# Decay bias by matmul, swapped keys out of the transpose, and one transpose of the probabilities per item, in an attention, SwiGLU and top-1 expert kernel

## The chip, the cores and the metric

The kernel runs on one core of a Trainium2 chip. The time is device microseconds (us) of one execution; the kernel before was timed three times. The profile is that of one further execution.

## What is computed

The inputs of the attention are q, k and v of 4 batches, 8 heads, 576 positions and 64 columns, and a decay f per position. The reference, cut to what matters:

```python
scores = scale * np.matmul(q, k.transpose(0, 1, 3, 2))
cum = np.cumsum(np.log(np.clip(f, 0.0001, 1.0)), axis=-1)
decay = cum[:, :, :, None] - cum[:, :, None, :]
scores = np.where(causal, -1000000000.0, scores + decay)
attn = softmax(scores)
x = np.matmul(attn, v)            # 2304 tokens of 512
x = (silu(x @ w_gate) * (x @ w_val)) @ w_out
x = top1_moe(x, gate, w1, w2)     # 8 experts
```

Within a row of the softmax the term of the query position is a constant, so only the term of the key position has to be subtracted from the scores.

## The kernel before

**Three stretches.** The attention goes by pairs of heads (16 pairs, 4 in each batch). Each pair has four items (`items`, L236): two heads times two groups of query rows; group 0 has the row blocks 0 to 2 and group 1 the row blocks 3 and 4. A slot (`slot`, L439) issues part 1 of item i, part 2 of item i-1 and the product with v of item i-2, and, by its place in the pair, the preparation of the next pair. In the first stretch (18 slots, about 165 us) the slots are mixed with the decoding and splitting of the weights, which come as 8-byte numbers. In the middle stretch (to about 612 us) the 46 slots left are mixed with units of the SwiGLU layer (`unit_g`, `unit_v`, `unit_o`), at a pace that `pace` (L1119) sets. After it come the remaining units, the routing and the experts, which the change doesn't touch.

**Order.** Every engine takes its instructions in the order of its own queue. That order is chosen when the kernel is built, by a planner that estimates when each instruction could start. All plain transfers and all DMA transposes of the attention are issued from the queue of SP.

**Preparation of a head** (`prep`, L200). q and k are scaled to f16 and split in a high and a low part: for each of the two, ScalarE writes the high part (L207) and VectorE the rest (L208). One DMA transpose (L210) turns the 10 blocks of 128 x 128 into `qkt`, with the high parts in partitions 0 to 63 and the low ones in 64 to 127. For the cross products high times low, VectorE copies the two halves of the transposed keys to swapped partitions (`ksw`, L214 and L215). The cumulated log decay of the head is fetched from `cum_d` in HBM, spread over 128 partitions by the transfer (`cb`, L218, 288 KB), and GpSimd multiplies it by the scale of the pair (L219).

**Part 1** (`part1`, L260). For each of the three column ranges of an item, `score` (L240) makes two matmuls, one with `qkt` (L244) and one with `ksw` (L246). In the first three batches (`inner`) a third one (L250) adds the causal mask of the diagonal block. VectorE then subtracts `cb` and takes the row maximum in one pass (L310). In the last batch there is no mask matmul: GpSimd adds the mask to `cb` for the diagonal blocks (L290), and the pass is cut in two where the diagonal block starts. ScalarE makes the bias of the exponential (L316) and the exponentials (L320).

**Part 2** (`part2`, L333). VectorE rounds the probabilities to f16 (L342), GpSimd makes the rest of the split (L345, L356), and a DMA transpose (L359) turns them: one of 9 blocks for an item of group 0, two of 7 and 9 blocks for an item of group 1. There are four f16 buffers of 9 blocks (`p16s`) and three transposed ones (`pt`).

**Product with v** (`pv`, L364): 40 matmuls per head (L380), each with one transposed block as the weights.

Of the kernel before, what the change touches and what calls it, by code (L numbers as in the profile page):

```python
# [7 lines left out]
F32 = mybir.dt.float32  # L8
# [13 lines left out]
MB = 3  # L22
# [6 lines left out]
def kernel(  # L29
# [36 lines left out]
    cum_d = dram.tile([B * H, S], F32, name="cum_d")  # L66
# [8 lines left out]
    masked = const.tile([128, 128], BF16, name="masked")  # L75
# [8 lines left out]
    rg = const.tile([128, KD, 32], F32, name="rg")  # L84
    sel = const.tile([128, NE], F32, name="sel")
# [11 lines left out]
    def consts():  # L97
# [5 lines left out]
        vec.tensor_scalar(out=masked, in0=maskgt, scalar1=-MASKED, scalar2=None, op0=ALU.mult)  # L103
# [18 lines left out]
        vec.tensor_single_scalar(out=sel, in_=sel_i, scalar=0.0, op=ALU.is_equal)  # L122
        vec.memset(rg, 0.0)
# [20 lines left out]
    NQK, NV, NPB, NBLK = 3, 1, 4, 9  # L144
# [6 lines left out]
    cb_p = at.enter_context(tc.tile_pool(name="cb", bufs=2))  # L151
# [4 lines left out]
    pt_p = at.enter_context(tc.tile_pool(name="pt", bufs=3))  # L156
# [24 lines left out]
    def scales(P):  # L181
        am = st_p.tile([128, 2], F32, tag="am", bufs=2, name="am")
        jk = qks_p.tile([128, 2, NCH, 2, D], F16, tag="qks", name="jk")
# [12 lines left out]
        stt[P] = (sc, c)  # L196
# [3 lines left out]
    def prep(P, hh):  # L200
        sc, c = stt[P]
        qks = qks_p.tile([128, 2, NCH, 2, D], F16, tag="qks", name="qks")
        for a in range(2):
            src = qk_in[(2 * P + a) % NQK][:, hh]
            s1 = sc[:, 0, a:a + 1]
            hi, lo = qks[:, a, :, 0, :], qks[:, a, :, 1, :]
# [3 lines left out]
        sp.dma_start_transpose(  # L210
            out=qkt.rearrange("p a (c t) -> p (a c) t", t=128), in_=qks.rearrange("p a c h d -> p (a c h d)")
        )
# [3 lines left out]
        cb = cb_p.tile([128, S], F32, tag="cb", name="cb")  # L216
        b, h = P // NP, 2 * (P % NP) + hh
        sp.dma_start(out=cb, in_=cum_d[b * H + h:b * H + h + 1, :].to_broadcast([128, S]))  # L218
        gp.tensor_tensor(out=cb, in0=cb, in1=c[:, 1:2].to_broadcast([128, S]), op=ALU.mult)  # L219
        heads[P, hh] = (qkt, ksw, cb)  # L220
# [19 lines left out]
    def score(ps, o, hd, j, k0, k1, inner):  # L240
        qkt, ksw, _ = hd
# [3 lines left out]
        d0, d1 = max(k0, 128 * j), k1 if inner else max(k0, 128 * j)  # L245
# [3 lines left out]
        if d1 > d0:  # L249
            pe.matmul(  # L250
                out=ps[:, o + d0 - k0:o + d1 - k0], lhsT=negid, rhs=maskgt[:, d0 - 128 * j:d1 - 128 * j],
                start=False, stop=True, skip_group_check=True,
            )
# [3 lines left out]

    stile = {}

    def part1(i):  # L260
        P, (hh, g) = i // 4, items[i % 4]
        hd = heads[P, hh]
        cb = hd[2]
        sc, c = stt[P]
        mx = st_p.tile([128, 8], F32, tag="mx", name="mx")
        inner = P < MB * NP
# [19 lines left out]
        if not inner:  # L286
            for m in range(nt):
                k0 = max(64, 128 * (base + m))
                k1 = 128 * (base + m) + 128
                gp.tensor_tensor(  # L290
                    out=sts[m][:, k0 - 64:k1 - 64], in0=cb[:, k0 - 64:k1 - 64], in1=masked[:, k0 - k1 + 128:], op=ALU.add
                )
        for grp in groups:
            ps = ps_s.tile([128, 512], F32, tag="s", name="ps")
            o = 0
            for j, k0, k1 in grp:
                score(ps, o, hd, j, k0, k1, inner)
                o += k1 - k0
            o = 0
            for j, k0, k1 in grp:  # L300
# [3 lines left out]
                d0 = k1 if inner else min(max(k0, 128 * j), k1)  # L304
                for a, b, bias in ((k0, d0, cb), (d0, k1, sts[m])):
                    if a < b:
                        left[m] -= b - a
                        x = m if not left[m] else nx
                        nx += left[m] > 0
                        vec.tensor_tensor_reduce(  # L310
                            out=sts[m][:, a - 64:b - 64], in0=ps[:, o + a - k0:o + b - k0], in1=bias[:, a - 64:b - 64],
                            scale=1.0, scalar=init, op0=ALU.subtract, op1=ALU.max, accum_out=mx[:, x:x + 1],
                        )
                        init = seen[m] = mx[:, x:x + 1]
# [13 lines left out]
    def p16_of(i, m):  # L328
        n, g = 6 * (i // 4), items[i % 4][1]
        n += i % 4 if g == 0 else 2 * (i % 4 - 1) + m  # L330
        return p16s[n % NPB].rearrange("p a t -> p (a t)"), 128 * OFF[m] if g == 0 else 0

    def part2(i):  # L333
# [4 lines left out]
        for ms in SUB[g]:  # L338
# [1094 lines left out]
```

## Time and profile before

| what | value |
|---|---|
| median of 3 runs | 1080.13 us (1072.58 to 1081.8) |
| the profiled execution | 1090.63 us |
| its span in the profile | 1088.5 us |
| TensorE busy | 880.6 us, 81% of the span |
| VectorE busy | 677.0 us, 62% |
| ScalarE busy | 537.0 us, 49% |
| GpSimd busy | 458.3 us, 42% |
| moved by DMA | 149.55 MB |

In the profile PE is TensorE's matmuls, PEld its weight loads, DVE is VectorE, ACT ScalarE, POOL GpSimd; SPq is the queue of SP, which issues transfers. L310 is line 310 of the kernel. A duration of one matmul includes its passage through the array, so matmuls overlap; how far apart they start tells what one costs.

### The profile page before, as it was taken

The page shows a single profiled execution, that of the slowest core. Times are in us where ns is not written, and L with a number is a line of the kernel's source. Part 1 is how long each engine was busy: PE and PEld are TensorE (multiplying, and loading weights), DVE is VectorE, ACT ScalarE, POOL GpSimd, SP SyncE. Part 2 cuts the span into 40 slices and gives each one's busy share as a digit, 9 for nine tenths or more (in the row PEclk, how much of TensorE's full clock was granted, in tenths as well). Part 3 has the DMA queues.
Part 4 walks back from the last instruction along what each step waited for, and adds up shares of the span by engine and source line. Part 5 has one row for each costly group of instructions (what it writes and reads, how often), then busy time and mean ns, then how long its engine had stood idle before and what let it go on. Part 6 is the DMA issues. An engine that isn't in the chain of part 4 may idle for free. (4 is left out here: it accounts for less than half of the span.)

```text
span 1088.5 us, 19531 instructions
## 1 busy us (share of the span) xinstructions
PE 880.6 (81%) x6789; PEld 726.5 (67%) x6789; DVE 677.0 (62%) x1946; ACT 537.0 (49%) x1160; POOL 458.3 (42%) x544
## 2 busy tenths in 40 slices
PE   1444448887976859899788899999877998999995
PEld 1333337765855648677667678888767887898994
DVE  4899799586675757777587542233334776665450
ACT  5877778464555636546264332222213645554441
POOL 2487676555344634466477412222215732110111
PEclk9995558998987979999989999999988999999998
DMA  8899889257778897767567360102328996555420
GB/s 222 186 228 221 189 171 216 63 121 158 166 102 155 144 127 155 148 108 147 84 103 155 45 194 11 40 1 39 59 48 207 255 218 190 167 181 164 173 100 31
DMA packets 298584, 149.55 MB, mean 137 GB/s; under 512 B 259697, under 2 KB 272113, under 8 KB 298484
## 3 DMA queue, kind: packets, MB, share of 16 engines
q1 hardware_dynamic: 294144, 137.83, 57.7%
q0 software_dynamic: 4096, 10.24, 3.9%
q8 instruction: 54, 0.88, 0.4%
q14 instruction: 46, 0.38, 0.2%
q10 hardware_dynamic: 244, 0.22, 0.1%
HBM read 91.06 MB, written 10.38 MB: 93 GB/s over the span
## 5 line engine op out<-in xcount | busy, mean ns | idle before, releaser
L490 PE MATMUL g<-xr,wg 128*128 128x256 f16 x1296 | 166.4, 282 | 18.9 <-ACT xr L433 10.5
L490 PE MATMUL v<-xr,wv 128*128 128x256 f16 x1296 | 170.1, 283 | 1.8 <-DVE t L523 1.2
L490 PEld LDWEIGHTS <-wv 128*128 128x128 f16 x1296 | 129.6, 103 | 32.9 <-issue 11.4
L490 PEld LDWEIGHTS <-wg 128*128 128x128 f16 x1296 | 125.1, 101 | 38.3 <-issue 16.9
L345 POOL TENSOR_TENSOR p<-st,p 128x128 f16<-128x128 f32 (+3 forms) x128 | 111.9, 880 | 45.1 <-DVE p L342 34.8
L530 POOL TENSOR_TENSOR lo<-t,hi 128x512 fp32r<-128x512 f32 x54 | 71.1, 1316 | 138.4 <-ACT hi L529 123.3
L380 PE MATMUL px<-vs,pt 128*128 128x64 f16 x1280 | 62.8, 207 | 65.1 <-DMA pt<-p 56.8
L380 PEld LDWEIGHTS <-pt 128*128 128x128 f16 x1280 | 55.6, 108 | 80.8 <-DMA pt<-p 64.2
L320 ACT ACTIVATE st<-st,nb,c 128x64 f32<-128x64 f32 (+4 forms) x160 | 102.7, 643 | 2.0
L342 DVE CAST p<-st 128x64 f16<-128x64 f32 (+4 forms) x160 | 74.4, 484 | 19.7 <-ACT st L320 16.2
L356 POOL TENSOR_TENSOR p<-st,p 128x64 f16<-128x64 f32 (+1 forms) x128 | 57.0, 448 | 54.0 <-issue 34.7
L529 ACT ACTIVATE hi<-t 128x512 fp32r<-128x512 f32 x54 | 33.7, 624 | 85.1 <-DVE t L523 85.1
L977 POOL DMA_INDIRECT out_dram<-o,ix x24 | 25.4, 1057 | 114.9 <-ACT o L1216 71.4
L244 PE MATMUL ps<-qkt 128*128 128x64 f16 (+3 forms) x192 | 54.6, 316 | 20.7 <-DVE mx L310 14.6
L1214 PE MATMUL bank<-whi,h 128*128 128x512 f32 x200 | 66.8, 399 | 3.7 <-ACT h L1176 2.9
L513 ACT ACTIVATE t<-g,gscale 128x512 f32<-128x512 f32 (+3 forms) x72 | 39.3, 570 | 60.2 <-PE g L490 60.1
L516 DVE SCALAR_TENSOR_TENSOR t<-t,g 128x512 f32<-128x512 f32 x54 | 36.8, 681 | 47.2 <-ACT t L513 45.4
L943 DVE TENSOR_TENSOR wlo<-wr,whi 128x1024 fp32r<-128x1024 f32 x48 | 57.6, 1244 | 13.7 <-ACT whi L942 12.9
L219 POOL TENSOR_TENSOR cb<-cb,c 128x576 f32<-128x576 f32 x32 | 38.5, 1204 | 61.2 <-DMA cb<-cum_d 53.5
L543 PE MATMUL yp<-wohi,hi 128*128 128x512 f32 x144 | 60.0, 417 | 0.0
L1171 PE MATMUL bank<-xh,whi 128*128 128x320 f32 (+1 forms) x192 | 59.4, 312 | 0.5 <-ACT xh L93 0.5
L246 PE MATMUL ps<-ksw,qkt 128*128 128x64 f16 (+2 forms) x192 | 56.5, 318 | 4.0 <-DVE ksw L215 3.9
(295 smaller groups left out, 2295.1 us busy)
## 6 DMA issues: line engine op xcount, KB each, us to landing
wr<-in_moe_w_dram SPq DMA_DIRECT2D x72, 512.0 KB, 5.0
cb<-cum_d SPq DMA_DIRECT2D x32, 288.0 KB, 4.3
vr<-in_v_dram SPq DMA_DIRECT2D x16, 288.0 KB, 4.9
qk_in<-in_q_dram SPq DMA_DIRECT2D x32, 128.0 KB, 2.7
qk_in<-in_k_dram SPq DMA_DIRECT2D x32, 128.0 KB, 3.0
v_in<-in_v_dram SPq DMA_DIRECT2D x32, 128.0 KB, 3.8
y_d<-ys SPq DMA_DIRECT2D x6, 512.0 KB, 3.4
wg<-in_moe_w_gate_dram SPq DMA_DIRECT2D x5, 512.0 KB, 4.4
```

Source lines behind the costliest of these rows:

```text
L246: pe.matmul(out=ps[:, o:o + n], lhsT=lq, rhs=ksw[:, k0 - 64:k1 - 64], start=False, stop=(d1 <= d0), skip_group_check=True)
L320: act.activation(out=sts[m], in_=sts[m], func=ACTF.Exp, scale=c[:, 0:1], bias=nb[:, m:m + 1], accum_out=sm[:, m, hh:hh + 1],)
L342: vec.tensor_copy(out=flat[:, o + 64:o + 64 + n], in_=src)
L345: gp.tensor_tensor(out=flat[:, o1:o1 + n - 64], in0=src[:, 64:n], in1=flat[:, o + 128:o + 64 + n], op=ALU.subtract)
L356: gp.tensor_tensor(out=blk[:, :, 0:64], in0=pair, in1=blk[:, :, 64:128], op=ALU.subtract)
L380: pe.matmul(out=px[:, 128 * m + 64 * hh:128 * m + 64 * hh + 64], lhsT=pm[:, o + ph * last + c, :], rhs=vs[:, hh, c, vh, :], start=(c == 0 ...
L490: pe.matmul(out=ps[:, fi, :], lhsT=w16[:, j, kk, wi, 128 * fi:128 * fi + 128], rhs=xr[:, kk, x0:x0 + 2, xi, :], start=(n_ == 0), stop=(n_ ...
L530: last["lo"] = gp.tensor_tensor(out=lo, in0=t, in1=hi.bitcast(F32), op=ALU.subtract)
L543: pe.matmul(out=yps[g][i], lhsT=hx[:, fi, 128 * i:128 * i + 128], rhs=wo[fk][wx], start=(j == 0 and n_ == 0), stop=(j == KF // 2 - 1 and n ...
L943: (eng or vec).tensor_tensor(out=l_, in0=t, in1=h_.bitcast(F32), op=ALU.subtract)
L1171: pe.matmul(out=p, lhsT=w[wi][:, kk, 128 * fk:128 * fk + 128], rhs=x[xi][:, kk, c0:CAP], start=(n_ == 0), stop=(n_ == 3 * KD - 1),)
L1214: pe.matmul(out=p[0:m, :], lhsT=hx, rhs=wx, start=(n_ == 0), stop=(n_ == len(prods) - 1))
```

## The change

The decay no longer goes through HBM. At the start the cumulated decay is split in three bf16 parts and laid out in `cum3`, 96 of 128 partitions: part i of head h of all 32 in partition 32 i + h. For each pair ScalarE makes `nc`, 128 x 256 in bf16, which holds minus the scale of the pair in the three partitions of each of the two heads and zero elsewhere. `score` makes one more matmul per column range, with `nc` of the head as the weights and `cum3` as the columns. The pass of VectorE stays, with a constant zero in place of `cb`. The mask matmul is now made in all four batches, and GpSimd's addition of the mask goes.

The swapped copy of the keys is now written ahead of the transpose: ScalarE writes the high part of the keys twice in one instruction, and one more ScalarE instruction copies the low part. The transpose has 15 blocks instead of 10; the copies L214 and L215 go.

The probabilities of an item lie in one buffer of 16 blocks, and one transpose turns them: 9 blocks for group 0, 16 for group 1. There are two f16 buffers and two transposed ones.

```diff
-    cum_d = dram.tile([B * H, S], F32, name="cum_d")
+    cum3 = const.tile([128, S], BF16, name="cum3")
+    pick = const.tile([128, B * H], F32, name="pick")
+    zero = const.tile([128, 1], F32, name="zero")
-    NQK, NV, NPB, NBLK = 3, 1, 4, 9
+    NQK, NV, NPB, NBLK = 3, 1, 2, 16
-    cb_p = at.enter_context(tc.tile_pool(name="cb", bufs=2))
-    pt_p = at.enter_context(tc.tile_pool(name="pt", bufs=3))
+    pt_p = at.enter_context(tc.tile_pool(name="pt", bufs=2))
...
+        act.activation(
+            out=nc_, in_=pick[:, h0:h0 + 2].rearrange("p (h o) -> p h o", o=1).to_broadcast([128, 2, 128]),
+            func=ACTF.Copy, scale=c[:, 1:2],
+        )
...
-            act.activation(out=hi, in_=src, func=ACTF.Copy, scale=s1)
+            act.activation(
+                out=part(w, w + D, 2) if n > 1 else hi, func=ACTF.Copy, scale=s1,
+                in_=src.rearrange("p (o c) d -> p o c d", o=1).to_broadcast([128, 2, NCH, D]) if n > 1 else src,
+            )
             vec.scalar_tensor_tensor(out=lo, in0=src, scalar=s1, in1=hi, op0=ALU.mult, op1=ALU.subtract)
-        qkt = qkt_p.tile([128, 2, NCH * 128], F16, tag="qkt", name="qkt")
-        ksw = qkt_p.tile([128, S], F16, tag="ksw", name="ksw")
-        vec.tensor_copy(out=ksw[0:64, :], in_=qkt[64:128, 1, 64:])
-        vec.tensor_copy(out=ksw[64:128, :], in_=qkt[0:64, 1, 64:])
-        sp.dma_start(out=cb, in_=cum_d[b * H + h:b * H + h + 1, :].to_broadcast([128, S]))
-        gp.tensor_tensor(out=cb, in0=cb, in1=c[:, 1:2].to_broadcast([128, S]), op=ALU.mult)
+        act.activation(out=qks[:, 2 * NCH:, 0, :], in_=lo, func=ACTF.Copy)
+        qkt = qkt_p.tile([128, 3, NCH * 128], F16, tag="qkt", name="qkt")
+        sp.dma_start_transpose(out=qkt.rearrange("p a (c t) -> p (a c) t", t=128), in_=flat)
...
+        pe.matmul(out=ps[:, o:o + n], lhsT=lq, rhs=qkt[:, 2, k0:k1], start=False, stop=False, skip_group_check=True)
         pe.matmul(
-            out=ps[:, o:o + n], lhsT=lq, rhs=ksw[:, k0 - 64:k1 - 64], start=False, stop=(d1 <= d0), skip_group_check=True
+            out=ps[:, o:o + n], lhsT=pk, rhs=cum3[:, k0 - 64:k1 - 64], start=False, stop=(k1 <= d0),
+            skip_group_check=True,
         )
...
+                vec.tensor_tensor_reduce(
+                    out=sts[m][:, k0 - 64:k1 - 64], in0=ps[:, o:o + n], in1=zero.to_broadcast([128, n]),
+                    scale=1.0, scalar=init, op0=ALU.subtract, op1=ALU.max, accum_out=mx[:, x:x + 1],
+                )
...
-            nblk = 9 if len(ms) > 1 else 2 * (base + ms[0]) + 1
-            pt = pt_p.tile([128, NBLK, 128], F16, tag="pt", name="pt")
-            sp.dma_start_transpose(out=pt[:, 0:nblk, :], in_=flat[:, 0:128 * nblk])
-            pts[P, hh, g] += [(pt, OFF[m] if g == 0 else 0) for m in ms]
+        nblk = 16 if g else 9
+        pt = pt_p.tile([128, NBLK, 128], F16, tag="pt", name="pt")
+        sp.dma_start_transpose(out=pt[:, 0:nblk, :], in_=flat[:, 0:128 * nblk])
+        pts[P, hh, g] = [(pt, p16_of(i, m)[1] // 128) for m in range(len(sts))]
...
-        act.dma_start(out=cum_d, in_=fz)
+        for i in range(3):
+            hi = c_p.tile([128, S], BF16, tag="c", name="cumhi")[0:B * H]
+            vec.tensor_copy(out=hi, in_=fz)
+            vec.tensor_copy(out=cum3[B * H * i:B * H * i + B * H, :], in_=fz)
+            if i < 2:
+                vec.tensor_tensor(out=fz, in0=fz, in1=hi, op=ALU.subtract)
```

## Rows read from the trace of the kernel before

**Rows 1.** Windows, the first two stretches: length, engines' busy time (instructions), clock, DMA share, GB/s.

```profile
0.00:165.00 165.00, 67.03 (x521) 47.58 (x521) 135.40 (x388) 121.51 (x296) 103.59 (x114) 0.78 0.89 204
165.00:612.00 447.00, 377.08 (x3533) 302.63 (x3533) 322.24 (x1062) 239.43 (x603) 237.38 (x319) 0.92 0.71 132
```

**Rows 2.** Waits of PE in the middle stretch: us in total, times, longest.

```profile
PE px L380 <- DMA pt<-p: 35.4, 18, 11.0
PE ps L244 <- DVE mx L310: 11.0, 8, 4.6
...
PE ps L246 <- DVE ksw L215: 2.4, 2, 2.2
```

**Rows 3.** Waits of DVE, then of POOL, in the middle stretch.

```profile
DVE ksw L214 <- DMA qkt<-qks: 37.7, 10, 9.8
...
POOL cb L219 <- DMA cb<-cum_d: 41.7, 12, 6.8
```

**Rows 4.** Timeline, 301 to 312 us: start, us, what [idle before <- releaser].

```profile
301.63 1.36 SPq L210 DMA_TRANSPOSE qkt<-qks  x1
...
309.30 0.30 DVE L214 COPY ksw<-qkt 64x576 f16<-64x576 f16 x1 [6.58 <-DMA qkt<-qks]
...
310.44 0.91 POOL L345 TENSOR_TENSOR p<-st,p 128x384 f16<-128x384 f32 x1 [6.93 <-DVE p L342]
...
310.92 0.56 PE L770 MATMUL tot<-am,onesf 128*128 128x2 f32 x2 [6.01 <-DVE mx L310]
```

**Rows 5.** Timeline, other idle times of PE in the middle stretch, and of POOL.

```profile
328.27 1.15 POOL L219 TENSOR_TENSOR cb<-cb,c 128x576 f32<-128x576 f32 x1 [4.94 <-DMA cb<-cum_d]
...
333.96 0.77 PE L380 MATMUL px<-vs,pt 128*128 128x64 f16 x11 [5.45 <-DMA pt<-p]
...
401.29 0.55 PE L380 MATMUL px<-vs,pt 128*128 128x64 f16 x7 [11.03 <-DMA pt<-p]
...
546.26 0.61 PE L244 MATMUL ps<-qkt 128*128 128x512 f16 x1 [4.62 <-DVE mx L310]
```

**Rows 6.** Groups by line, whole span: busy us, mean ns, idle before and releasers.

```profile
L208 DVE SCALAR_TENSOR_TENSOR qks<-qk_in,sc,qks 128x320 f16<-128x320 f32 x64 | 43.9, 725 | 2.1 <-ACT qks L207 2.1
...
L219 POOL TENSOR_TENSOR cb<-cb,c 128x576 f32<-128x576 f32 x32 | 38.5, 1204 | 61.2 <-DMA cb<-cum_d 53.5 <-PE ps L246 4.5 <-DVE ys L574 2.5
...
L207 ACT ACTIVATE qks<-qk_in,sc 128x320 f16<-128x320 f32 x64 | 30.8, 549 | 8.4 <-DVE sc L780 8.4
...
L185 ACT ACTIVATE jk<-qk_in 128x640 f16<-128x640 f32 x32 | 23.3, 729 | 39.6 <-DMA qk_in<-in_k_dram 21.9 <-DMA qkt<-qks 15.6 <-DVE fz L756 1.8
...
L214 DVE COPY ksw<-qkt 64x576 f16<-64x576 f16 x32 | 18.5, 580 | 44.7 <-DMA qkt<-qks 44.1
...
L290 POOL TENSOR_TENSOR st<-cb,masked 128x128 f32<-128x128 f32 (+1 forms) x40 | 16.6, 443 | 0.1
...
L215 DVE COPY ksw<-qkt 64x576 f16<-64x576 f16 x32 | 12.7, 396 | 0.5
```

**Rows 7.** Timeline of PE, two score matmuls of 512 columns in a row.

```profile
318.97 0.38 PE L244 MATMUL ps<-qkt 128*128 128x512 f16 x1
319.19 0.38 PE L246 MATMUL ps<-ksw,qkt 128*128 128x512 f16 x1
```

**Rows 8.** Windows, two stretches of 40 us, columns as in rows 1.

```profile
40.00:80.00 40.00, 19.01 (x135) 12.24 (x136) 36.52 (x102) 30.07 (x73) 32.18 (x33) 1.00 1.00 222
...
360.00:400.00 40.00, 26.38 (x296) 21.01 (x293) 27.02 (x107) 20.08 (x55) 20.04 (x26) 0.90 0.90 115
```

**Rows 9.** DMA issues: count, KB each, median us from issue to landing.

```profile
cb<-cum_d SPq DMA_DIRECT2D x32, 288.0 KB, 4.3
...
pt<-p SPq DMA_TRANSPOSE x96, 3.4
...
qkt<-qks SPq DMA_TRANSPOSE x32, 3.6
```

**Rows 10.** Windows, a stretch with the clock at half, columns as in rows 1.

```profile
306.90:317.10 10.20, 6.18 (x26) 4.95 (x27) 7.24 (x28) 3.47 (x11) 6.21 (x9) 0.50 0.35 57
```

More of the change, by code (lines that the diff above doesn't have):

```diff
@@ L21 @@
 MASKED = -float(2 ** 100)
-MB = 3
 EXP1 = 1 << 23
@@ L122, in consts @@
         vec.tensor_single_scalar(out=sel, in_=sel_i, scalar=0.0, op=ALU.is_equal)
+        pick_i = c_p.tile([128, B * H], I32, tag="c", name="pick_i")
+        gp.iota(pick_i, [[-1, B * H]], base=0, channel_multiplier=1)
+        vec.tensor_single_scalar(out=pick_i, in_=pick_i, scalar=B * H - 1, op=ALU.bitwise_and)
+        vec.tensor_scalar(out=pick, in0=pick_i, scalar1=0.0, scalar2=-1.0, op0=ALU.is_equal, op1=ALU.mult)
+        vec.memset(cum3, 0.0)
+        vec.memset(zero, 0.0)
         vec.memset(rg, 0.0)
@@ L201, in prep, with part @@
         sc, c = stt[P]
-        qks = qks_p.tile([128, 2, NCH, 2, D], F16, tag="qks", name="qks")
-        for a in range(2):
+        qks = qks_p.tile([128, 3 * NCH, 2, D], F16, tag="qks", name="qks")
+        flat = qks.rearrange("p c h d -> p (c h d)")
+        w = 2 * NCH * D
+        def part(o, step, n):
+            dims = [list(flat.ap[0])] + ([[step, n]] if n > 1 else []) + [[2 * D, NCH], [1, D]]
+            return type(flat)(flat.tensor, flat.offset + o, dims)
+        for a, n in ((0, 1), (1, 2)):
             src = qk_in[(2 * P + a) % NQK][:, hh]
             s1 = sc[:, 0, a:a + 1]
-            hi, lo = qks[:, a, :, 0, :], qks[:, a, :, 1, :]
-            act.activation(out=hi, in_=src, func=ACTF.Copy, scale=s1)
-            vec.scalar_tensor_tensor(out=lo, in0=src, scalar=s1, in1=hi, op0=ALU.mult, op1=ALU.subtract)
-        qkt = qkt_p.tile([128, 2, NCH * 128], F16, tag="qkt", name="qkt")
-        sp.dma_start_transpose(
-            out=qkt.rearrange("p a (c t) -> p (a c) t", t=128), in_=qks.rearrange("p a c h d -> p (a c h d)")
-        )
-        ksw = qkt_p.tile([128, S], F16, tag="ksw", name="ksw")
-        vec.tensor_copy(out=ksw[0:64, :], in_=qkt[64:128, 1, 64:])
-        vec.tensor_copy(out=ksw[64:128, :], in_=qkt[0:64, 1, 64:])
-        cb = cb_p.tile([128, S], F32, tag="cb", name="cb")
-        b, h = P // NP, 2 * (P % NP) + hh
-        sp.dma_start(out=cb, in_=cum_d[b * H + h:b * H + h + 1, :].to_broadcast([128, S]))
-        gp.tensor_tensor(out=cb, in0=cb, in1=c[:, 1:2].to_broadcast([128, S]), op=ALU.mult)
-        heads[P, hh] = (qkt, ksw, cb)
+            hi, lo = [qks[:, NCH * a:NCH * a + NCH, x, :] for x in range(2)]
+            act.activation(
+                out=part(w, w + D, 2) if n > 1 else hi, func=ACTF.Copy, scale=s1,
+                in_=src.rearrange("p (o c) d -> p o c d", o=1).to_broadcast([128, 2, NCH, D]) if n > 1 else src,
+            )
+            vec.scalar_tensor_tensor(out=lo, in0=src, scalar=s1, in1=hi, op0=ALU.mult, op1=ALU.subtract)
+        act.activation(out=qks[:, 2 * NCH:, 0, :], in_=lo, func=ACTF.Copy)
+        qkt = qkt_p.tile([128, 3, NCH * 128], F16, tag="qkt", name="qkt")
+        sp.dma_start_transpose(out=qkt.rearrange("p a (c t) -> p (a c) t", t=128), in_=flat)
+        heads[P, hh] = (qkt, c[1][:, hh, :])
     vsp = {}
@@ L238, with score @@
     sums = {}
-    def score(ps, o, hd, j, k0, k1, inner):
-        qkt, ksw, _ = hd
+    def score(ps, o, hd, j, k0, k1):
+        qkt, pk = hd
         n = k1 - k0
@@ L244, in score @@
         pe.matmul(out=ps[:, o:o + n], lhsT=lq, rhs=qkt[:, 1, k0:k1], start=True, stop=False, skip_group_check=True)
[L245 removed]
+        pe.matmul(out=ps[:, o:o + n], lhsT=lq, rhs=qkt[:, 2, k0:k1], start=False, stop=False, skip_group_check=True)
+        d0 = max(k0, 128 * j)
         pe.matmul(
[L247 removed]
+            out=ps[:, o:o + n], lhsT=pk, rhs=cum3[:, k0 - 64:k1 - 64], start=False, stop=(k1 <= d0),
+            skip_group_check=True,
         )
[L249 removed]
+        if k1 > d0:
             pe.matmul(
[L251 removed]
+                out=ps[:, o + d0 - k0:o + k1 - k0], lhsT=negid, rhs=maskgt[:, d0 - 128 * j:k1 - 128 * j],
                 start=False, stop=True, skip_group_check=True,
@@ L285, in part1 @@
         seen, left, nx = {}, [x.shape[1] for x in sts], nt
[L286 to L292, printed above, removed]
         for grp in groups:
@@ L296, in part1 @@
             for j, k0, k1 in grp:
-                score(ps, o, hd, j, k0, k1, inner)
+                score(ps, o, hd, j, k0, k1)
                 o += k1 - k0
@@ L303, in part1 @@
                 init = seen.get(m, -3e38)
[L304 to L314, printed above, removed]
+                left[m] -= n
+                x = m if not left[m] else nx
+                nx += left[m] > 0
+                vec.tensor_tensor_reduce(
+                    out=sts[m][:, k0 - 64:k1 - 64], in0=ps[:, o:o + n], in1=zero.to_broadcast([128, n]),
+                    scale=1.0, scalar=init, op0=ALU.subtract, op1=ALU.max, accum_out=mx[:, x:x + 1],
+                )
+                seen[m] = mx[:, x:x + 1]
                 o += n
```

16 lines of the change are left out of this document (6 added, 10 removed).

## The prediction

> **What bounds the kernel now.** I read the windows by stretch first, since the attention, which is all that the change touches, ends at about 612 us. In the first stretch VectorE is busy for 135 of 165 us and the DMA engines for 0.89 of it, while TensorE has 67 us [rows 1]: VectorE and the transfers set the pace. In the middle stretch TensorE is busy for 377 of 447 us and VectorE for 322 [rows 1]: TensorE's queue sets the pace, and its 70 us of idle time is all that can be gained there. The last stretch, the 476 us left of the span, runs code that stays.
>
> Then the waits of TensorE in the middle stretch: half of the 70 us, 35.4, is for transposed probabilities, and 11.0 for VectorE's maximum before a score [rows 2]. Then what VectorE and GpSimd wait for, as both stand in the chain in front of those: VectorE stood for 37.7 us in the copy of the swapped keys, until the transpose of the keys landed, and GpSimd for 41.7 us until `cb` landed [rows 3]. These are waits at the head of a queue. The copy isn't urgent, since it serves the next head, but all that stands behind it waits too. The timeline shows one whole case: a key transpose issued at 301.63 lets VectorE go on at 309.30; the cast behind the copy comes late, so GpSimd idles 6.93 us; the maximum behind it comes late, so TensorE idles 6.01 us [rows 4]. A second goes through GpSimd (4.94 us for `cb`, then TensorE 5.45 us for `pt`) and a third ends in 4.62 us before a score [rows 5]. The longest, 11.03 us, waits for a transpose itself [rows 5]; no engine's queue explains that one, so I leave it where it is.
>
> **The change part by part.**
>
> *Bias by matmul, on TensorE.* Two score matmuls of 512 columns start 0.22 us apart [rows 7]. A head has 64 + 192 + 320 + 448 + 64 + 512 = 1600 columns, so 1600 / 512 x 0.22 = 0.69 us. Of the 32 heads 22 are prepared in the middle stretch: 15.1 us. The mask matmuls of the last batch are 64 + 128 + 128 + 128 + 64 = 512 columns for each of 8 heads: 0.22 x 8 = 1.8 us. Together 17 us. In the first stretch TensorE idles more than half of the time and the 10 heads there, 7 us at full clock, cost nothing; without that cover they would cost 7 to 14. In the middle stretch TensorE is busy for 377 / 447 = 0.84 of the time, so I count 0.84 x 17 = +14 us, between 0 and +17.
>
> *The decay off HBM, GpSimd and SP.* 32 multiplications of 1204 ns (38.5 us) and 40 mask additions (16.6 us) leave GpSimd, and so does the wait for `cb` [rows 3, 6]. The new pass of VectorE reads a constant in place of `cb`: the same elements, so the same time; the 32 extra pieces of the last batch go with the mask. The split of the decay at the start is eight VectorE instructions on 32 partitions before the first score, in place of a write to HBM and a read back of 4.3 us [rows 9]: no difference.
>
> *Swapped keys.* The copies, 580 + 396 ns, leave VectorE: 0.98 us x 32 = 31 us [rows 6], and with them its wait. What is late next is TensorE itself, at the first score of the next head, with nothing due before. ScalarE gets, per head, 729 - 549 = 0.18 us for the doubled high part (the row of 640 elements against that of 320) and a copy of 0.55 us, 23 us in all, and per pair the 256 elements of `nc`, taken at 0.4 us, 6 us. The copy of the low part waits for VectorE (725 ns [rows 6]), and behind it in ScalarE's queue stand the exponentials. ScalarE is busy 239 of 447 us in the middle stretch, so I take this as hidden there; what it costs without cover is a rival below.
>
> *The transposes.* The trace has none of 15 or 16 blocks. The nearest are 10 blocks, 3.6 us to landing, and 7 or 9, 3.4 us [rows 9]. One of 16 lies between 3.4 (no cost per block) and 6.8 us (two after each other); from 8 to 10 blocks the step is 0.2 us, 0.1 per block, which gives 4.1 for 15 and 4.2 for 16, and I take that. For an item of group 1 the product can no longer start on the first half while the second is made: about 1 us later when TensorE waits for it, and of its 18 waits for `pt` [rows 2] I give half to group 1, of which a third stays on the path: +3 us, between 0 and +10. SP issues 32 transposes and 32 transfers less. With two buffers instead of three, an item's transpose waits for the product of the item two before it; an item of group 1 took two of the three before, so that wait isn't new.
>
> *The DMA engines.* The change adds 5 x 32 = 160 blocks of 32.8 KB, 5.2 MB, and takes 9.4 MB of `cb` away. A stretch with many transposes moved 115 GB/s at 0.90 busy, one with many plain transfers 222 at 1.00 [rows 8]; so a transposed byte costs 222 / 128 = 1.7 plain ones, and the two cancel: 0 us. The Trainium skill says otherwise (Advanced Engine Details and Errata, section X-Bar Transpose (TRN2)): transposing transfers on trn2 are as fast as others. By that, 4.2 MB would be saved, 1.3 MB of it in the first stretch, an estimate of 6 us at 222 GB/s, and the sum would come out at 1058. The rows speak against it.
>
> *What is gained.* First stretch: 10 x 0.98 = 9.8 us leave the busiest engine; the DMA engines, full from 40 to 80 us [rows 8], give nothing back; I take half, -5 us, between 0 and -10. Middle stretch: the three cases above, 6.0 + 5.4 + 4.6, and one of 2.2 us at the swapped keys themselves [rows 2]: -18 us, between 0 and, if the same queues stand behind the other small ones, -35. TensorE runs at half clock after such gaps: from 306.9 to 317.1 the granted clock is 0.50, the level of 1.2 GHz, and 6.18 us of matmuls there [rows 10] would take 3.1; twice that for the two long cases, -6 us, between 0 and -10. A chain that is shorter by GpSimd's 1.2 us per head, and free of its waits, -4 us, between 0 and -15.
>
> Sum: +14 + 3 - 5 - 18 - 6 - 4 = -16 us. The profiled execution took 1090.63 us, 2.1 us of it outside its span, so 1074.6 after; it lies 10.5 us above the median of the runs shown, so the median goes from 1080 to 1064 us.
>
> **The rivals.**
>
> *The waits only move: no change.* What holds `pt` back is the landing of transposes, not the queues: the 11.03 us case and most of the 35.4 us stay, and a freed VectorE meets the same late transposes. For it: the key transpose of rows 4 took 7.7 us against a median of 3.6, so the transfers were late themselves. Against it: in that case TensorE waited for VectorE, and not for `pt`. Only 6 of the 18 us and the 5 of the first stretch come back, and the clock 2: +14 + 3 - 13 = +4, 1080 to 1084 us.
>
> *ScalarE holds the exponentials back: slower.* The copy of the low part stands at the head of ScalarE's queue until VectorE has made it. Price: up to two remainders of 0.73 and the copies of 0.73, 2.2 us per head, in 22 heads 48 us. It decides where more than 16 / 22 = 0.7 us of it per head comes through to `pt`; at 1.5 us it is +33, 1097 us. For it: in the first stretch ScalarE is busy 121 of 165 us [rows 1]. Against it: the half-idle ScalarE of the middle stretch, and a planner that can put the copy later.
>
> *The gaps close.* If without these queue heads half of the 70 us go, and the clock with them, -35 - 10 + 17 - 10 = -38: 1042 us. For it: each long gap of rows 4 and 5 but one has VectorE's or GpSimd's wait in it. Against it: the smaller gaps have many causes.
>
> **How the numbers follow.** The forecast has 0.43, the gaps closed 0.15, no change 0.24, slower 0.18. The forecast's own range, with half of the ends of its terms, is 1050 to 1074. A change of over 1%, 10.8 us, is what a measurement of this kernel can tell from none; the forecast gives 0.40 of its chance to faster and 0.03 to the same. So faster 0.55, same 0.27, slower 0.18. The range takes in the gaps closed and most of the slower case: 1036 to 1096 us.
>
> **What would show it.** Right: no wait of VectorE for `qkt`, no wait of GpSimd for `cb`; TensorE's idle time in the middle stretch down by about 20 us, with a third score row of the same length as L246; ScalarE up by some 29 us in all. Wrong: waits for `pt` of 35 us or more, key or probability transposes that land later than 4.2 us on average, or waits of ScalarE in the preparation with TensorE idle behind them.

## The result, and the profile after

The changed kernel takes 1044.98 us (median of 4 runs, 1041.6 to 1046.13); the kernel before, run beside it, 1080.91 (4 runs, 1072.58 to 1081.8). The ratio is 0.9679, with a 95% interval of 0.9626 to 0.9732: 35 us less. The sign is as forecast and the time lies in the range, but the forecast was 16 us: the number is that of the rival in which the gaps close (1042). The profiled execution took 1045.53 us (span 1043.6), near its median; that of before lay 10 us above its own, so the traces differ by 45 us where the medians differ by 36.

The windows of the changed kernel, to set against [rows 1] (length, busy us and instructions of PE, PEld, DVE, ACT and POOL, granted clock, DMA share, GB/s):

```profile
0.00:165.00 165.00, 74.63 (x582) 53.95 (x589) 146.26 (x413) 139.08 (x339) 98.90 (x115) 0.77 0.94 215
165.00:592.00 427.00, 389.77 (x3756) 316.70 (x3775) 273.19 (x930) 248.39 (x617) 191.20 (x253) 0.96 0.66 125
```

To compare equal work, I cut every trace at four marks that any order has: the first matmuls of the 2nd, the 36th and the 54th SwiGLU unit (`g<-xr,wg`, 24 matmuls to a unit), and the end. Worked out from each trace, in us, with the time in which TensorE was idle in the middle part (its length less TensorE's busy time in it):

| kernel | to 2nd | middle, 2nd to 36th | of it idle | to 54th | rest |
|---|---|---|---|---|---|
| before | 174.8 | 453.3 | 71.3 | 152.6 | 307.8 |
| changed | 180.1 | 411.9 | 30.2 | 152.0 | 299.6 |

The two middle parts, first before, then changed, as windows:

```profile
174.80:628.10 453.30, 382.00 (x3565) 306.66 (x3565) 317.38 (x1056) 236.05 (x596) 235.62 (x316) 0.93 0.69 126
```
```profile
180.10:592.00 411.90, 381.72 (x3672) 310.04 (x3691) 261.46 (x911) 238.51 (x594) 179.15 (x241) 0.97 0.66 124
```

The middle is 41 us shorter, and all 41 are idle time of TensorE (the expectation for e12, below, says 39). Its busy time is the same, although the bias matmuls are in it: the granted clock rose from 0.93 to 0.97. VectorE and GpSimd are each relieved of some 56 us there.

The waits of TensorE in the changed kernel's middle (us in total, times, longest), which answer to [rows 2]:

```profile
PE tot L774 <- ACT jk L189: 8.8, 2, 7.9
PE ps L256 <- DMA qkt<-qks: 7.5, 5, 4.7
...
PE px L379 <- DMA pt<-p: 5.7, 8, 1.1
```

The wait for transposed probabilities fell from 35.4 us in 18 to 5.7 in 8. VectorE's and GpSimd's waits of [rows 3] have no row any more; GpSimd now waits for VectorE's cast, and the longest entry of VectorE is a wait for TensorE itself (`st` is the pass over the scores):

```profile
DVE st L311 <- PE ps L264: 21.7, 12, 6.1
...
POOL p L344 <- DVE p L341: 56.3, 34, 11.2
```

What was added is as foreseen. On the timeline the third score matmul of 512 columns starts 0.22 us after the second [rows 7]; ScalarE's groups by line, beside [rows 6], show the copy of the low part at 459 ns and `nc` at 493. The first of them holds the single high part of q beside the doubled one of the keys, 681 ns on average instead of 549; with q's still at 548, the doubled one takes 813:

```profile
305.71 0.38 PE L256 MATMUL ps<-qkt 128*128 128x512 f16 x1
305.93 0.38 PE L257 MATMUL ps<-qkt 128*128 128x512 f16 x1
306.15 0.38 PE L259 MATMUL ps<-cum,nc 128*128 128x512 bf16 x1
```
```profile
L224 ACT ACTIVATE qks<-qk_in,sc 128x320 f16<-128x320 f32 x64 | 39.7, 681 | 4.0 <-DVE sc L784 2.1 <-DMA qkt<-qks 1.9
...
L229 ACT ACTIVATE qks<-qks 128x320 f16<-128x320 f16 x32 | 14.4, 459 | 6.8 <-DVE qks L228 6.7
...
L202 ACT ACTIVATE nc<-pick,c 128x256 bf16<-128x256 f32 x16 | 7.9, 493 | 0.0
```

### The profile page after: what moved, and what is told of

Same layout as the page of the kernel before. It is cut to its first block, busy times and chain, and to the rows that moved or that the text cites. A ratio compares the mean times of both kernels' runs of the same rounds, so it can differ in the third digit from the quotient of the medians.

```text
span 1043.6 us, 19717 instructions
## 1 busy us (share of the span) xinstructions
PE 884.5 (85%) x7003; PEld 735.8 (71%) x7029; DVE 635.3 (61%) x1829; ACT 559.2 (54%) x1208; POOL 402.1 (39%) x473
## 5 line engine op out<-in xcount | busy, mean ns | idle before, releaser
L489 PE MATMUL g<-xr,wg 128*128 128x256 f16 x1296 | 159.3, 276 | 11.0 <-ACT xr L432 6.5
L489 PE MATMUL v<-xr,wv 128*128 128x256 f16 x1296 | 162.1, 279 | 0.0
L344 POOL TENSOR_TENSOR p<-st,p 128x128 f16<-128x128 f32 (+3 forms) x128 | 109.4, 860 | 83.8 <-DVE p L341 62.9
L379 PE MATMUL px<-vs,pt 128*128 128x64 f16 x1280 | 54.5, 202 | 33.6 <-DMA pt<-p 22.0
L256 PE MATMUL ps<-qkt 128*128 128x64 f16 (+2 forms) x192 | 56.7, 313 | 29.2 <-DMA qkt<-qks 25.9
L379 PEld LDWEIGHTS <-pt 128*128 128x128 f16 x1280 | 49.0, 105 | 45.0 <-DMA pt<-p 27.6
L311 DVE CUSTOM_DVE_ANT_0 st<-ps,zero 128x64 f32<-128x64 f32 (+3 forms) x160 | 55.4, 375 | 23.8 <-PE ps L264 23.3
L528 ACT ACTIVATE hi<-t 128x512 fp32r<-128x512 f32 x54 | 33.8, 626 | 62.1 <-DVE t L522 62.0
L257 PE MATMUL ps<-qkt 128*128 128x64 f16 (+2 forms) x192 | 60.3, 316 | 0.0
```

Of the source, the lines that this page charges most:

```text
L257: pe.matmul(out=ps[:, o:o + n], lhsT=lq, rhs=qkt[:, 2, k0:k1], start=False, stop=False, skip_group_check=True)
L344: gp.tensor_tensor(out=flat[:, o1:o1 + n - 64], in0=src[:, 64:n], in1=flat[:, o + 128:o + 64 + n], op=ALU.subtract)
L379: pe.matmul(out=px[:, 128 * m + 64 * hh:128 * m + 64 * hh + 64], lhsT=pm[:, o + ph * last + c, :], rhs=vs[:, hh, c, vh, :], start=(c == 0 ...
L489: pe.matmul(out=ps[:, fi, :], lhsT=w16[:, j, kk, wi, 128 * fi:128 * fi + 128], rhs=xr[:, kk, x0:x0 + 2, xi, :], start=(n_ == 0), stop=(n_ ...
```

## The experiments

**The parts.** The change has three parts; each kernel is the changed code with parts put back to the old lines. The swapped keys alone weren't tried.

| label | bias | keys | one transpose | ratio, 95% | to 2nd | middle | idle | rest |
|---|---|---|---|---|---|---|---|---|
| e1 | no | no | yes | 0.9984 (0.9957 to 1.0011) | 173.9 | 442.3 | 66.8 | 307.6 |
| e2 | yes | no | no | 0.9813 (0.9759 to 0.9867) | 185.3 | 417.2 | 36.2 | 298.1 |
| e3 | yes | yes | no | 0.9600 (0.9542 to 0.9657) | 166.8 | 412.8 | 32.2 | 300.5 |
| e4 | yes | no | yes | 0.9831 (0.9776 to 0.9886) | 190.9 | 414.2 | 33.8 | 299.1 |

The edit of e1 is the last hunk of the diff (buffers and transpose), with `cb` and `ksw` as before:

```diff
-    NQK, NV, NPB, NBLK = 3, 1, 4, 9
+    NQK, NV, NPB, NBLK = 3, 1, 2, 16
...
-    pt_p = at.enter_context(tc.tile_pool(name="pt", bufs=3))
+    pt_p = at.enter_context(tc.tile_pool(name="pt", bufs=2))
```

> The kernel before with one transpose of the probabilities per item, 16-block f16 and transposed buffers two deep; decay and keys as before. Theory Q (the gain comes from the waits at the heads of the queues of VectorE and GpSimd, which stay here): between -0.4 and +0.6%, waits of TensorE for pt in the middle stretch still about 30 us. Rival T (fewer, larger transposes and the new buffers let the probabilities land earlier): 1.5 to 2.5% faster, waits for pt down to 10 to 15 us.

e2 takes `cum3`, `pick`, `nc` and the third matmul and leaves the rest:

```diff
-        sp.dma_start(out=cb, in_=cum_d[b * H + h:b * H + h + 1, :].to_broadcast([128, S]))
-        gp.tensor_tensor(out=cb, in0=cb, in1=c[:, 1:2].to_broadcast([128, S]), op=ALU.mult)
...
+            out=ps[:, o:o + n], lhsT=pk, rhs=cum3[:, k0 - 64:k1 - 64], start=False, stop=(k1 <= d0),
```

> The kernel before with the bias by matmul and the mask matmul in all batches; keys and transposes of the probabilities as before. Theory Q: GpSimd's 41.7 us of waits for cb go, VectorE's 37.7 us for the transposed keys stay: 1.2 to 2.2% faster. Rival T: the 17 us of matmuls are paid and nothing is won on pt: from 0.5% faster to 1% slower.

e3 is the changed kernel with four f16 buffers of 9 blocks, three transposed ones and two transposes per item of group 1; e4 is the changed kernel with the copies `ksw` on VectorE:

```diff
-    NQK, NV, NPB, NBLK = 3, 1, 2, 16
+    NQK, NV, NPB, NBLK = 3, 1, 4, 9
```

> The changed kernel with the transposes and buffers of the probabilities as before (two transposes for an item of group 1, four and three buffers of 9 blocks). Theory Q: within 0.5% of the changed kernel, so 2.7 to 3.7% faster than before. Rival T: 0.7 to 1.7% faster than before, waits for pt 25 us or more.

```diff
-        act.activation(out=qks[:, 2 * NCH:, 0, :], in_=lo, func=ACTF.Copy)
+        vec.tensor_copy(out=ksw[0:64, :], in_=qkt[64:128, 1, 64:])
+        vec.tensor_copy(out=ksw[64:128, :], in_=qkt[0:64, 1, 64:])
```

> The changed kernel with the swapped keys copied by VectorE after the transpose, as before (transpose of 10 blocks). Theory Q: VectorE's wait for the transposed keys is back, about 35 us, and half of the gain of the middle stretch with it: 1.2 to 2.2% faster than before. Rival T: within 0.5% of the changed kernel, 2.7 to 3.7% faster than before.

The bias alone brings the middle from 453 to 417 us, nearly all that the middle gains. VectorE's wait for the swapped keys, which I had put at the head of the story, is still there in e2, longer than before, and TensorE's wait for the probabilities is gone all the same. In e2's middle the waits of VectorE and of TensorE read:

```profile
DVE ksw L254 <- DMA qkt<-qks: 44.9, 19, 6.0
```
```profile
PE px L436 <- DMA pt<-p: 9.8, 10, 1.5
```

In the kernels with `cb` and its multiplication TensorE's waits for `pt` in the middle are 38.7 us (before; 35.4 in the window of [rows 2]), 33.8 (e11, the same kernel in another order, below) and 23.5 (e1, for which theory Q had about 30 and its rival 10 to 15; the ratio is Q's).

The keys, on top of it, bring 2.1% (e2 to e3), 18.5 of the 20.8 us between the spans ahead of the second unit. e4 says the same: its ratio is where theory Q had it, but not for Q's reason, as VectorE's wait for the keys is back (36.0 us) and the middle stays at 414 us; what it loses lies ahead of the second unit. The one transpose brings nothing alone (e1) and costs on top of the rest (e3 to changed): e3 is faster than either theory had it.

**Is it the wait or the work?** One theory was that engines standing at the head of their queue for a transfer were the cost; its rival, that it was the work itself. Two kernels put work back without a transfer to wait for. e5 is e2 with a multiplication of GpSimd per head on a constant tile, the size of that of `cb`; e6 is e3, whose keys ScalarE swaps, with three copies of VectorE per head that move as much as the old two. What they write is not used.

```diff
+        gp.tensor_tensor(out=idle, in0=idle, in1=c[0][:, 1:2].to_broadcast([128, S]), op=ALU.mult)
```

> The kernel of the bias alone, with GpSimd made to multiply 128x576 numbers per head again, from a constant tile that no transfer writes: the work of L219 without its wait; the product is used nowhere. Theory Q (the wait for cb at the head of GpSimd's queue was the cost): within 0.5% of the bias alone, ratio to before 0.976 to 0.986. Rival W (GpSimd's 38 us of work were the cost): half of the gain lost, ratio 0.989 or more.

```diff
+        for z in range(3):
+            vec.tensor_copy(out=idle[0:64, :], in_=flat[64:128, 640 + 384 * z:1024 + 384 * z])
```

> The changed kernel with two transposes as before, with VectorE made to copy as many f16 numbers per head as for the swapped keys, from the tile ahead of the transpose, so without a wait for the transfer; the copy is used nowhere. Theory Q: within 0.5% of the same kernel without the copies, ratio to before 0.955 to 0.965. Rival W (VectorE's 31 us of work were the cost): 0.971 or more.

e5: 0.9965 (0.9938 to 0.9993) against e2's 0.9813; 6.8 us more to the second unit, 15.5 more in the middle. e6: 0.9789 (0.9756 to 0.9822) against e3's 0.9600; 22 us more to the second unit (14 against e14, which is e3 in another order), 7 in the middle. Neither work had a transfer to wait for; e5's multiplication waited 2.3 us in the middle for the pair's scale. For the keys the work is the cost: e6 gives back 20 of the 23 us that the keys gain by the ratios, most of it in the first stretch, which VectorE fills. GpSimd's work alone is worth 16 us.

The middles of e2 and e5, as windows, show a second way in which GpSimd's work can cost:

```profile
185.30:602.50 417.20, 380.99 (x3685) 309.82 (x3706) 267.14 (x957) 227.61 (x574) 178.61 (x241) 0.98 0.58 115
192.10:624.80 432.70, 389.51 (x3683) 314.80 (x3702) 283.99 (x957) 226.81 (x573) 202.94 (x262) 0.96 0.59 110
```

VectorE executes as many instructions and is busy for 17 us more. Half of that is in the 40 splits of q and k (`qks`), 876 ns on average in e5 against 667 in e2; in e5 those with GpSimd idle take 541 ns and those beside the added multiplication 1217. So the added work both stands ahead of GpSimd's remainders and lengthens what VectorE does beside it. How the 16 us divide between the two no run separates; in the kernel before these splits take 695 ns, so e5 may price the old multiplication too high.

**The transfer by itself.** e9 is e2 with the write of `cum_d` and the transfer of `cb` put back, and no reader.

```diff
+        cb = cb_p.tile([128, S], F32, tag="cb", name="cb")
+        sp.dma_start(out=cb, in_=cum_d[b * H + h:b * H + h + 1, :].to_broadcast([128, S]))
```

> The bias alone (0.981), with the write of the cumulated decay to HBM and, per head, the 288-KB transfer of it to 128 partitions put back on the queue of SP, into a buffer that no engine reads (one buffer instead of two; what is written is not used). GpSimd's multiplication and its wait stay away. GpSimd's work without the transfer cost 15.5 us of the middle stretch, of the 36 us that the bias alone gains there; this run shows where the rest lies. Theory T (the transfer itself holds up the transposes that stand behind it in the queue of SP or on the DMA engines): TensorE's waits for the transposed probabilities in the middle stretch rise from 9.8 us to 20 or more, the middle stretch from 417 to 428 or more, and the whole is at 0.990 to 1.000. Theory Q (it was GpSimd's wait at the head of its queue, together with its work): the middle stretch stays within 6 us of 417, the waits for the probabilities stay below 15 us, and the whole is at 0.978 to 0.987. For the end stretch, whose code the bias doesn't touch but which took 298 instead of 308 us in all kernels without the write: if the place of the buffers in HBM behind it decides, it goes back to 305 or more here.

0.9897 (0.9834 to 0.9961), 1068.37 us, 9 us above e2 by the ratios; the middle rose to 441.1 us with 51.6 idle. The two intervals overlap, so the 9 us may be anything from near 0 to 18; but the four runs of e9 (1066.31 to 1072.4 us) all lie above the four of e2 (1053.54 to 1058.18). So the transfer costs by itself, as theory T had it, but the ratio falls just short of T's bounds and the path is not T's: the waits for probabilities stay at 5.0 us, and what grew is TensorE's wait for VectorE's maximum, behind VectorE's copy of the keys. The timeline shows the longest one, about half of the growth in idle time:

```profile
307.52 1.52 SPq L248 DMA_TRANSPOSE qkt<-qks  x1
...
318.40 0.30 DVE L253 COPY ksw<-qkt 64x576 f16<-64x576 f16 x1 [9.31 <-DMA qkt<-qks]
...
320.31 0.21 PE L282 MATMUL ps<-qkt 128*128 128x64 f16 x1 [7.72 <-DVE mx L353]
```

That is the case of [rows 4] again. Since this profile holds one such rare long landing (the last section returns to it), the 24 us of its middle overstate the transfer; the 9 us of the ratios are the better size. With e5's 16 they make 25, if the two add. The bias alone gains 20 net, with the 15 of its matmuls (e7, below) already paid, so some 35 in all, an estimate from these ratios; the 10 left (the mask additions, GpSimd's wait itself, or work and transfer together) weren't tried and are no more than the intervals leave open.

**The sizes of two terms.** e7 makes the bias matmul twice with half the value; e8 cuts the transpose of an item of group 1 into its two halves again, on the new buffers.

```diff
-        pe.matmul(
+        for z in range(2):
+            pe.matmul(
```

> The changed kernel with each bias matmul made twice at half the scale: 51200 columns more, 22 us at full clock, 15 us of them in the middle stretch. If TensorE's queue paces the middle stretch, as forecast, 0.84 to 0.95 of the 15 us show: ratio to before 0.979 to 0.985 (the changed kernel: 0.968). If the matmuls run in idle time: under 0.973.

```diff
-        sp.dma_start_transpose(out=pt[:, 0:nblk, :], in_=flat[:, 0:128 * nblk])
+            a, z = ((0, 7), (7, 16))[ms[0]] if g else (0, 9)
+            sp.dma_start_transpose(out=pt[:, a:z, :], in_=flat[:, 128 * a:128 * z])
```

> The changed kernel with its buffers of 16 blocks two deep, but with two transposes into them for an item of group 1, of 7 and 9 blocks, the first as soon as its row block is ready. If one transpose per item costs by its late start, the ratio to before is that of the kernel with the old transposes, 0.957 to 0.964. If the old buffers were the better ones, it stays at 0.966 to 0.971.

e7: 0.9819 (0.9783 to 0.9856), 15 us more than the changed kernel, from 8 to 22 by the intervals: the price of one bias matmul per column range. e8: 0.9668 (0.9634 to 0.9702), no different from the changed kernel: starting the product on the first half gains nothing that shows, and no run of e8 (1040.17 to 1044.95 us) is as short as the longest of e3 (1036.78). So the late start is at most a small part of what the one transpose costs.

**What costs with one transpose.** e13 is e3 with three f16 buffers instead of four: room for two items, as the changed kernel has.

```diff
-    NQK, NV, NPB, NBLK = 3, 1, 4, 9
+    NQK, NV, NPB, NBLK = 3, 1, 3, 9
```

> The bias and the swapped keys without the one transpose (0.960), with three f16 buffers of 9 blocks instead of four: room for two items (one of each group), as the changed kernel has with its two buffers of 16 blocks. Transposed buffers stay three of 9 blocks, room for two items as well. The one transpose per item cost 13 us beside the other two parts, and cutting it in two on the same buffers brought nothing back. Theory B (the depth of the f16 buffers: the cast waits until the transpose of the item two before it has been read): here 0.965 to 0.973, with VectorE waiting for a transpose in the cast, 5 us or more in the middle stretch. Theory O (order and shape: the depth is not it): 0.955 to 0.963.

0.9714 (0.9654 to 0.9774): within theory B, but it doesn't show the depth to be the cost. One of its four runs is long (1054.88 us; the others 1039.92 to 1044.64), the interval overlaps e3's, and the planner wrote another order: about a quarter of VectorE's instructions stand elsewhere than in e3. e14, below, is e3 in another order with all four buffers, and its trace looks like that of e13: 175.1 and 413.2 us against 174.5 and 415.1 in the first two columns of the table, 1037.3 and 1037.8 us in all. By the medians e13 is 5 us above e14 (1044.32 and 1038.83 us). VectorE's wait in the cast for a transpose to have read the buffer is 10.2 us in e13's middle and 10.3 in the changed kernel's, against 6.3 in e3, as theory B had it; but e8, with the buffers and the time of the changed kernel, has 4.4. That the depth costs is likely at best; by what the one transpose costs stays open.

**Controls.** Another step count of the weight decoding gives another order: e11 for the kernel before, e12 for the changed one, e14 for e3. In e11 about a quarter and in e14 a fifth of VectorE's instructions stand elsewhere, but in e12 almost none (the traces' orders agree in 99.7%), so e12 tests little. e10 tests whether the last stretch, 8 us shorter in the trace of the changed kernel though its code is the same, follows the place of its buffers in HBM.

```diff
-    PRE0, PRE = 2, 43
+    PRE0, PRE = 2, 42
```

> A control: the kernel before, with 42 instead of 43 steps of the weight decoding ahead of the attention's first slots, and nothing else changed. The planner then writes another order in the first stretch. It shows how much of a difference between two kernels comes from the order alone. If the order hardly matters, 0.996 to 1.004 and the milestones within 3 us of those of the kernel before; if it matters as much as the parts of the change do, a difference of 1 to 2% of either sign, and then no part whose effect is below that can be told from it.

> A control: the changed kernel with 42 instead of 43 steps of the weight decoding ahead of the attention's first slots. As for the kernel before: 0.964 to 0.972 if the order hardly matters; 0.955 to 0.980 outside that if it does. The middle stretch should stay at 405 to 418 us either way, since 39 us of idle time left it and an order of the first stretch can't bring them back; a middle stretch above 425 would say that the gain was the order's.

> A control for the fastest kernel, the bias and the swapped keys without the one transpose (0.960), with 42 instead of 43 steps of the weight decoding ahead of the attention's first slots, as was tried for the kernel before and the changed one, where it made 0.003 or less. If the 13 us between this kernel and the changed one belong to the one transpose, it stays at 0.956 to 0.964; if they are luck of the order in the first stretch, where all of the 13 us lie, it moves to 0.966 or more.

```diff
+    cum_d = dram.tile([B * H, S], F32, name="cum_d")
     y_d = dram.tile([NT + 1, DM], F32, name="y_d")
...
+        act.dma_start(out=cum_d, in_=fz)
```

> The changed kernel with the buffer of the cumulated decay in HBM declared again ahead of the buffer of the expert outputs, and written once at the start; nothing reads it. If the end stretch (from the last SwiGLU units on) was 8 us shorter after the change because the expert outputs lie at another place in HBM, it goes back from 300 to 305 us or more and the whole to 0.972 to 0.976. If it was shorter for another reason (what the attention leaves in the queues, or the order), it stays at 296 to 302 and the whole at 0.965 to 0.971.

| label | ratio, 95% | to 2nd | middle | idle | rest |
|---|---|---|---|---|---|
| e11 | 1.0029 (1.0000 to 1.0058) | 177.2 | 445.5 | 62.4 | 305.4 |
| e12 | 0.9679 (0.9612 to 0.9746) | 176.7 | 413.2 | 30.1 | 303.7 |
| e14 | 0.9624 (0.9587 to 0.9661) | 175.1 | 413.2 | 32.0 | 298.1 |
| e10 | 0.9719 (0.9651 to 0.9786) | 180.7 | 412.3 | 31.3 | 300.7 |

In e11 and e14 the order moves the whole by 0.3% or less, and a single mark by up to 8 us; changed and e12, of almost the same order, differ by 3 us at the first mark. Every experiment on a part writes another order too, so a difference of 0.3% between two of them can't be told from that of the order. The middle of the kernels with `cb` and its multiplication is 442 to 453 us (e1, e11, before) and that of every kernel without `cb` and without work put back 409 to 417, in many orders: this gain is no matter of order. Its size is 30 to 41 us, and the trace of before, the longest of the three, gives the upper end. The last stretch isn't the place in HBM (e10: 300.7) and not the absence of the transfer (e9: 298.0); with the same code it takes 295.6 (e7) to 307.8 us, and why stays open. The 13 us by which e3 is ahead of the changed kernel at the second unit shrink to 5 in e14 (2 against e12), while its ratio hardly moves. So where the cost of the one transpose lies the traces don't show; by the ratios it is 0.0055 to 0.008, 6 to 9 us. Neither difference alone is well clear of its interval; but the eight runs of e3 and e14 (1040.11 us at most) are all shorter than the twelve of changed, e8 and e12 (1040.13 at least).

The bias and the swapped keys without the one transpose, e3, is the fastest kernel: 1031.88 us (median of 4), below the kernel before and the changed one.

## Why the prediction was right in sign and half in size

- **Bias by matmul, +14: right.** e7 measures 15 us by the ratios, with an interval from 8 to 22; in its trace the middle is 21 us longer. The columns were countable and a row gave their price.
- **The clock, -6: of the right size or too small.** Averaged over TensorE's busy time in the middle alone, the granted clock was 0.943 before and 0.975 after, which makes 360 and 372 us of work at full clock in the same 382 us. At 0.943 the 372 would have taken 395, so the clock gave back 13 us, about what the bias matmuls cost; against e11 (0.945) it is 12 and against e1 (0.958) 7. I had bounded it at 10. I counted the matmuls behind the two longest gaps; the clock stood at its lower level, 1.2 GHz, for 65 us of the middle before and for 27 after.
- **Middle gaps, -18: the term that failed.** It was mis-sized by half: TensorE's idle time fell by 41 us in the traces (by 32 to 37 from e11 or e1), about the outer end, -35, that I took for the rival. I added up three cases from the timeline and left the rest, and I put the 11.03 us wait for `pt` aside because no engine's queue explained it. But the waits for `pt` fell from 35.4 to 5.7 us, and from 33.8 in e11, whose longest is 6.6 us and not 11. What shrank them is the bias part alone (9.8 in e2), with the key copies still waiting. So the story told by [rows 4], the copy of the keys at the head of VectorE's queue, was the smaller cause in the middle: 417 to 413 us from e2 to e3.
- **The DMA engines, 0: wrong.** I traded `cb`'s bytes for transposed ones at a rate from two stretches, and so gave the transfer no price. e9 gives it 9 us by the ratios, uncertain by as much, without a single wait for `cb` itself. The one case shown there goes through a key transpose that lands late; whether the transfer makes it late isn't shown. By the Trainium skill (Advanced Engine Details and Errata, section X-Bar Transpose (TRN2)) transposing transfers are as fast as others, which would have made the sum 1058, an estimate. No run here measures the rate of transposed bytes by itself, and the result lies below either sum.
- **GpSimd's work, taken as nearly free behind its wait: wrong.** I named the wait as the harm (41.7 us) and gave 4 us to the shorter chain, up to 15 at the outer end. e5 shows the multiplication alone, with no transfer to wait for, at 16 us of the whole. GpSimd is busy for about half of the middle, but its remainder stands between each cast and its transpose, and a microsecond put ahead of it can delay that: with the work TensorE's waits for `pt` rise from 9.8 us in e2 to 15.7 in e5. The rest comes with VectorE's longer instructions and a lower clock.
- **Swapped keys in the first stretch, -5: too small.** e2 to e3 is 18.5 us to the second unit in the traces (10 against e14), and e6 puts 22 back with work alone (14 against e14). So copies of 20 x 0.5 us cost at least their whole busy time. I halved 9.8 us because the DMA engines were full; the stretch was VectorE's. The bias part, which I had called no difference there, has 10 us against it in e2 and hardly 3 in e9, so its part is not settled; the net of the changed kernel is +5 in the first two traces and 0 from e11 to e12. So none of the 5 us forecast for this stretch came in the whole change; its gain lies in the middle and, 8 us in these two traces and 2 from e11 to e12, in the last stretch, which I had as unchanged and where the cause is open.
- **The transposes, +3: near in size, wrong in reason.** It costs 6 to 9 us, and hardly by the late start (e8). I compared the transposed buffers, three against two, and found no new wait; the f16 buffers ahead of them, four of 9 blocks against two of 16, I didn't follow. Whether they are the reason e13 doesn't settle, so that stays open.
- **ScalarE, +29 hidden: right.** The three additions are 31 us in its groups (the doubling 0.26 us instead of 0.18, the copy 0.46 instead of 0.55, `nc` 0.49 instead of 0.4); its busy time rose by 22 us in the span, and its new wait (`qks` L229) is 6.7 us in all. The longest wait of TensorE does name it (`jk`, the squares of the next q and k, 7.9 us), but ScalarE had itself stood there for 12.8 us, for a load of the keys (last section), and not for VectorE. That rival fell.

The signs that I had named came out as the right ones (no waits for `cb` or `qkt` on GpSimd and VectorE, the third row, ScalarE up), but the idle time fell by twice the 20 us announced. The landing of the larger transposes, one of the signs of being wrong, can't be read from the profile after, which gives no landing times for them; in e8's the median of the key transposes of 15 blocks is 4.2 us, where 4.1 was estimated.

## What to carry to other kernels

Where one engine sets the pace and is idle for a sixth of a stretch, price its whole idle time against the chain that feeds it and not the few gaps that a timeline explains: the bias took two links out of that chain, and nearly half of the idle time went, with the clock behind it. Work of an engine at 50% is not free when it stands in the queue ahead of a link of that chain; test it by putting the work back without its wait. When buffers are exchanged for larger and fewer ones, follow every buffer of the chain in items, not only the one that is written last. And compare orders before a control of the order is believed: e12 changed a number in the kernel and next to nothing in the order.

## What was not expected of the hardware

The 11.03 us wait of [rows 5] is neither a queue of an engine nor a lack of bandwidth. The windows of before around it show the DMA engines as busy while next to nothing is moved (last two columns: DMA share and GB/s; over so short a window the share can pass 1), from 396 us on with every engine idle; the timeline shows that the probabilities, the scatter of the token numbers (`id_d`) and the keys, issued at 390.27, 389.50 and 391.70, all came free within a microsecond:

```profile
392.00:394.00 2.00, 0.00 (x0) 0.00 (x0) 0.46 (x1) 1.91 (x8) 0.62 (x2) 0.56 1.75 157
394.00:396.00 2.00, 0.00 (x0) 0.00 (x0) 0.00 (x0) 0.34 (x2) 0.00 (x0) 0.50 1.70 5
396.00:398.00 2.00, 0.00 (x0) 0.00 (x0) 0.00 (x0) 0.00 (x0) 0.00 (x0) 0.50 1.71 4
398.00:400.00 2.00, 0.00 (x0) 0.00 (x0) 0.00 (x0) 0.00 (x0) 0.00 (x0) 0.50 0.96 3
```
```profile
401.32 0.99 POOL L737 DMA_INDIRECT id_d<-tid,pos  x1 [8.70 <-DMA id_d<-tid,pos]
...
402.21 1.46 DVE L214 COPY ksw<-qkt 64x576 f16<-64x576 f16 x1 [9.76 <-DMA qkt<-qks]
```

The changed kernel has a shorter one with the same kinds of transfers in flight, and its longest wait of TensorE for the keys (4.74 us) is that:

```profile
373.00:375.00 2.00, 2.00 (x22) 1.85 (x20) 1.93 (x11) 1.97 (x6) 1.63 (x2) 1.00 1.45 6
```
```profile
380.52 0.23 PE L256 MATMUL ps<-qkt 128*128 128x64 f16 x1 [4.74 <-DMA qkt<-qks]
381.56 0.98 POOL L736 DMA_INDIRECT id_d<-tid,pos  x1 [5.94 <-DMA id_d<-tid,pos]
```

Its longest wait of all has the same neighbours. The queue of SP stood for 8.77 us in the issue of a key transpose, half a microsecond after a scatter had been issued, and ScalarE waited 12.80 us for a load of the next keys:

```profile
283.26 1.14 POOL L736 DMA_INDIRECT id_d<-tid,pos  x1 [1.64 <-DVE hscale L806]
283.82 8.77 SPq L231 DMA_TRANSPOSE qkt<-qks  x1
...
293.05 0.74 ACT L189 ACTIVATE jk<-qk_in 128x640 f16<-128x640 f32 x1 [12.80 <-DMA qk_in<-in_k_dram]
293.93 0.59 PE L774 MATMUL tot<-am,onesf 128*128 128x2 f32 x2 [7.91 <-ACT jk L189]
```

The long landing of e9 above is one more: a scatter issued at 308.00 and the key transpose issued at 307.52 come free together at 318.4. In each of these a scatter of single words is under way beside transposes, and what waits for the transfers shown stands for 5 to 13 us. Whether the scatter is the cause no run here separates; it is in the kernels with and without the change, and the 11.03 us of before may be why that execution lay 10 us above its median. What is left of TensorE's idle time in the changed kernel's middle has its two longest pieces there.
